# The middle column's product, six units later in a hand-written plan

## The chip, the cores and the metric

The kernel runs on one core of one Trainium2 chip. The metric is the device time of one execution in microseconds (us), the median of the runs shown.

## The reference

Inputs are q, k and v (8 batches, 8 heads, 576 positions, 64 channels, float32) and two feed-forward weights. What is computed:

```python
out_local = softmax(band(q k^T / 8, |i - j| < 4)) v
out_up    = repeat(softmax(qd kd^T / 8) vd, 4)
x     = (out_up + out_local).reshape(8, 576, 512)
mixed = real(fft(fft(x, axis=1), axis=2))
u     = x + mixed
un    = (u - mean(u)) / sqrt(var(u) + 1e-6)
out   = u + relu(un @ w_ch1) @ w_ch2
```

Here qd, kd and vd are means over groups of four positions (144 groups). The Fourier step is what the change touches: its real part is made of matmuls with cosine and sine tables, first along the sequence, then along the channels.

## The kernel before, in words

**Stages.** The work before the feed-forward goes batch by batch. `Unit` (five per batch, 40 in all) does the banded attention: `scores`, `maxima`, `exps`, `transpose_p`, `copy_p`, `values`, `result`. `Pooled` does the pooled attention in three parts per batch, from sums of q and k over four positions (`sum_in`, on VectorE and GpSimd) and sums of v (`sum_v`, on GpSimd, from loads of vsum). `Mix` does the Fourier step. `Block` (nine blocks of four tiles of 128 tokens) adds u together by DMA, normalizes it, turns it and runs the feed-forward; `Quarter` converts the 64-bit weights into pairs of float32r parts, in a chain of a load by SyncE, `size` on ScalarE (L190), `clamp` on GpSimd (L195), `join` on VectorE (L203 to L209), `high` on ScalarE (L220) and `low` on GpSimd or VectorE (L225).

**The Fourier step of a batch (class `Mix`).** The symmetry of the tables lets the kernel fold the channels: `cross` (L649, GpSimd) and `fold` (L659 and L660, VectorE) make sums and differences, `split_high` (L667, ScalarE) and `split_low` (L675, GpSimd, for the last fold VectorE) part each value into two float32r numbers. There are four slots of rows; slot 0 is folded last. `sequence(T)` for T = 0 to 3 (L695) is a wide product: twelve matmuls of 290 columns, of high and low parts of all four slots with the table seqm; slot 0 is the last of each four. `sequence_high` (L703) and `sequence_low` (L706) read its result. These are the four wide products.

The fold leaves out the middle column, number 256 of 512. `split_z` (L680 on VectorE, L683 on ScalarE, L684 on VectorE) puts it into the small tile z, high and low part side by side, so two columns of weights. `sequence_z` (L719) multiplies it with seqm in eight matmuls of 290 columns into a bank of PSUM; `z_high` (L722, ScalarE) and `z_low` (L725, VectorE) write it as rows 0 to 1 and 32 to 33 of the tile yz. The even half of `mix` (L741), the channel stage, reads yz in its last matmul.

**What sets the order.** Nothing is reordered by a compiler. Every step is put on a list with a time in units of a plan, `at(t, step)`; the list is sorted by these times (L1070) and issued in that order, which is the order on each engine's queue. A batch has 20 units (`PACE`). The times come from the table `AT` (L28 to L67); for the Fourier step they count from `mix_at(b)`, stretched by 1.21 for batch 0:

```python
            for d, fn in zip(AT["z"], (self.split_z, self.sequence_z, self.z_high, self.z_low)):
                at(t + pace * d, fn)
```

With `"sequence": (12.86, 2.15, 0.71, 1.85)` the four wide products stand at 12.86, 15.01, 17.16 and 19.31, their readers 0.71 and 1.85 behind each. The first value of `AT["z"]` also enters `t_a` (L988), the time from which the plan closes the attention's memory and starts the feed-forward; for the last batch `t_a` is 9.14 behind `mix_at`, so from there blocks of the feed-forward stand between its wide products.

**Banks of PSUM.** `bank()` (L278) gives each product the bank whose last reader has the earliest time in the plan. There are eight banks before `t_a` and four after it, the other four being the feed-forward's accumulators.

Of the kernel before, what the change touches and what calls it, by code (L numbers as in the profile page):

```python
# [35 lines left out]
    "crosses": ((1, 4.24), (2, 5.87), (0, 8.67)),  # L36
    "folds": ((3, 3.9), (1, 4.66), (2, 7.94), (0, 10.61)),
    "splits": (0.74, 1.58, 2.04),
    "z": (9.04, 9.92, 11.56, 13.75),
    "sequence": (12.86, 2.15, 0.71, 1.85),  # L40
    "mixed": (22.32, 2.54, 0.37, 0.41, 1.73, 2.46),
    "store_local": (6.68,),
# [1172 lines left out]
```

## Time and profile before

| what | value |
|---|---|
| median of 3 runs | 1126.36 us (1123.96 to 1127.71) |
| the profiled execution | 1122.9 us |
| its span | 1121.1 us, 20828 instructions |
| TensorE busy | 1076.5 us (96%) |
| VectorE busy | 527.6 us (47%) |
| ScalarE busy | 346.8 us (31%) |
| GpSimd busy | 347.0 us (31%) |
| mean granted clock of TensorE | 0.977 |

The span is the time from the first to the last instruction of the profiled execution; the rest of its time lies around it. In the profile PE is TensorE, PEld its weight loads, DVE VectorE, ACT ScalarE, POOL GpSimd, SP SyncE. [...] Batches 0 to 7 have their product of the middle column at 52.8, 82.4, 121.8, 162.0, 202.4, 239.1, 272.4 and 301.2 us.

### The profile page before, as it was taken

The numbers are of one execution on the slowest core, as the hardware profiler recorded it, in microseconds if no ns is written. First come the engines' busy times: TensorE is split into PE (matmuls) and PEld (weight loads), VectorE is DVE, ScalarE is ACT, GpSimd is POOL, SyncE is SP. The second block draws the span as 40 slices with busy tenths as digits, with TensorE's granted clock in tenths as the row PEclk, the third lists the DMA queues.
The fourth block names the chain that finished last, engine by engine and source line by source line (L and its number), as shares of the span: only waits on it lengthen the run. The fifth ranks groups of instructions, "written<-read, shape, count | busy, mean of one in ns | idle before, by whom it ended". The sixth has DMA issues, their size and how long they took to land.

```text
span 1121.1 us, 20828 instructions
## 1 busy us (share of the span) xinstructions
PE 1076.5 (96%) x8204; PEld 885.1 (79%) x8204; DVE 527.6 (47%) x1270; ACT 346.8 (31%) x1025; POOL 347.0 (31%) x473
## 2 busy tenths in 40 slices
PE   6899889989899999999999999999999999999998
PEld 5677667768788778888888888888888888888886
DVE  5889699888798884231321322322222232132111
ACT  5877566667444442111111111111111111111110
POOL 3555766664355564205003005004003201300000
PEclk8899799989999999999999999999999999999999
DMA  8777998874434444315007007005104302401001
GB/s 319 266 240 237 248 268 243 224 246 149 132 104 139 121 132 110 61 52 99 1 7 143 1 1 148 4 1 121 30 1 102 49 1 73 78 1 38 1 1 38
DMA packets 67550, 118.50 MB, mean 106 GB/s; under 512 B 8852, under 2 KB 25062, under 8 KB 67451
## 3 DMA queue, kind: packets, MB, share of 16 engines
q1 hardware_dynamic: 50986, 97.22, 26.8%
q0 software_dynamic: 16464, 19.93, 11.5%
q8 instruction: 65, 1.06, 0.4%
q14 instruction: 35, 0.28, 0.1%
HBM read 89.21 MB, written 27.65 MB: 104 GB/s over the span
## 4 chain that ended last, share of the span: by engine, by line
PE 74%; DVE 11%; DMA 6%; ACT 4%; issue 2%; POOL 1%; SPq 1%; ACTq 0%; DVEq 0%; POOLq 0%
PE hps L922 31%; PE acc L942 11%; PE acc L940 11%; PE acc L941 10%; DMA raw<-in_wq_dram 3%; PE y L695 2%; ACT sb L534 1%; PE mix L741 1%; DVE wt L206 1%; PE tpn L890 1%; DMA vsum<-in_vg_dram 1%; PE tpl L546 1%; PE sc L515 1%; PE av L563 1%; DVE mx L528 1%
## 5 line engine op out<-in xcount | busy, mean ns | idle before, releaser
L930 DVE SCALAR_TENSOR_TENSOR hl<-hps,hh 128x512 fp32r<-128x512 f32 x144 | 99.3, 690 | 461.9 <-ACT hh L926 461.9
L922 PE MATMUL hps<-unT,w1h 128*128 128x512 f32 x1152 | 311.4, 392 | 0.0
L922 PEld LDWEIGHTS hps<-unT,w1h 128*128 128x128 f32 x1152 | 215.0, 188 | 43.9
L926 ACT ACTIVATE hh<-hps 128x512 fp32r<-128x512 f32 x144 | 86.0, 598 | 503.9 <-PE hps L922 501.7
L940 PE MATMUL acc<-w2h,hh 128*128 128x512 f32 x576 | 225.5, 392 | 1.8 <-DVE ut L946 0.9
L942 PE MATMUL acc<-w2h,hl 128*128 128x512 f32 x576 | 224.6, 390 | 0.0
L941 PE MATMUL acc<-w2l,hh 128*128 128x512 f32 x576 | 224.2, 389 | 0.0
L922 PE MATMUL hps<-unT,w1l 128*128 128x512 f32 x576 | 154.4, 390 | 0.0
L940 PEld LDWEIGHTS acc<-w2h,hh 128*128 128x128 f32 x576 | 108.0, 188 | 25.1 <-DVE ut L946 1.3
L942 PEld LDWEIGHTS acc<-w2h,hl 128*128 128x128 f32 x576 | 108.1, 188 | 23.7 <-DVE hl L930 1.2
L922 PEld LDWEIGHTS hps<-unT,w1l 128*128 128x128 f32 x576 | 108.3, 188 | 23.1 <-POOL w1l L225 0.2
L941 PEld LDWEIGHTS acc<-w2l,hh 128*128 128x128 f32 x576 | 108.2, 188 | 22.0
L852 POOL DMA_DIRECT2D ut<-um x72 | 61.6, 1492 | 195.9 <-DMA ut<-ul 192.6
L875 POOL TENSOR_TENSOR rstd<-rstd,mhalf 128x1 f32<-128x1 f32 x36 | 20.0, 555 | 277.6 <-DVE rstd L874 275.7
L534 ACT ACTIVATE sb<-sc,mx 128x64 f32<-128x64 f32 x320 | 69.8, 329 | 1.3
L899 DVE TENSOR_TENSOR unT<-tpn,unT 128x512 fp32r<-128x512 f32 x36 | 24.8, 689 | 61.3 <-ACT unT L896 61.3
L332 POOL TENSOR_TENSOR vsum<-vsum 128x650 f32<-128x650 f32 x24 | 38.5, 1603 | 39.6 <-DMA vsum<-in_vg_dram 39.5
L896 ACT CAST unT<-tpn 128x512 fp32r<-128x512 f32 x36 | 21.2, 588 | 94.5 <-PE tpn L890 94.5
L190 ACT ACTIVATE wt<-raw 128x256 f32<-128x256 f32 x64 | 28.2, 441 | 67.7 <-DMA raw<-in_wq_dram 50.6
L695 PE MATMUL y<-seqm,fh 128*128 128x290 f32 (+1 forms) x256 | 43.7, 313 | 1.7 <-ACT fh L667 1.3
L839 POOL DMA_DIRECT2D ut<-ud x40 | 43.1, 1794 | 2.0 <-DMA ut<-um 1.8
L649 POOL TENSOR_TENSOR pq<-x 128x256 f32<-128x256 f32 x48 | 32.2, 700 | 28.5 <-issue 15.6
(110 smaller groups left out, 1344.7 us busy)
## 6 DMA issues: line engine op xcount, KB each, us to landing
qkT<-in_qk_dram SPq DMA_DIRECT2D x40, 512.0 KB
raw<-in_wq_dram SPq DMA_DIRECT2D x64, 256.0 KB
vsum<-in_vg_dram SPq DMA_DIRECT2D x32, 325.0 KB
vaug<-in_vw_dram SPq DMA_DIRECT2D x40, 260.0 KB
out_dram<-ut SPq DMA_DIRECT2D x36, 256.0 KB
ul<-x SPq DMA_DIRECT2D x8, 1024.0 KB
ut<-ud POOLq DMA_DIRECT2D x32, 256.0 KB, 6.2
ut<-um POOLq DMA_DIRECT2D x38, 128.0 KB, 4.5
```

Of the source, the lines that this page charges most:

```text
L332: eng.tensor_tensor(out=b, in0=a, in1=b, op=ALU.add)
L534: nc.scalar.activation(out=self.sb[:, hp, h2], in_=sc[:, hp], func=AF.Exp, scale=0.125, bias=self.mx[:, h2, hp : hp + 1],)
L649: nc.gpsimd.tensor_tensor(out=pq[:, i], in0=u[:, t, HD + 1 : DM + 1], in1=v[:, t, 0:HD], op=ALU.add)
L695: nc.tensor.matmul(y, l, r, start=(i == 0), stop=(i == len(mms) - 1))
L839: nc.gpsimd.dma_start(out=u[to : to + m], in_=groups, accum_op=ALU.add)
L852: nc.gpsimd.dma_start(out=u[to : to + m, h * HD : h * HD + HD], in_=um[b][i, k + j : k + j + m, z : z + HD], accum_op=ALU.add,)
L922: nc.tensor.matmul(hps, a[:, c, :], unT[:, x, c, :], start=(i == 0), stop=(i == len(mms) - 1))
L926: nc.scalar.activation(out=hh, in_=self.hps[f], func=AF.Relu)
L930: nc.vector.scalar_tensor_tensor(out=hl, in0=self.hps[f], scalar=0.0, in1=self.hh[f].bitcast(F32), op0=ALU.max, op1=ALU.subtract)
L940: nc.tensor.matmul(acc, hh, w2h, start=start, stop=False)
L941: nc.tensor.matmul(acc, hh, w2l, start=False, stop=False)
L942: nc.tensor.matmul(acc, hl, w2h, start=False, stop=stop)
```

## The change

Of the table `AT` the second, third and fourth time of "z" change. `sequence_z` moves from 9.92 to 15.8, `z_high` from 11.56 to 16.8 and `z_low` from 13.75 to 17.3; `split_z` keeps 9.04.

```diff
     "splits": (0.74, 1.58, 2.04),
-    "z": (9.04, 9.92, 11.56, 13.75),
+    "z": (9.04, 15.8, 16.8, 17.3),
     "sequence": (12.86, 2.15, 0.71, 1.85),
```

In each batch the eight matmuls of L719 then come between the second wide product (15.01) and the third (17.16), where they came ahead of the first (12.86). On ScalarE L722 comes behind the second wide product's L703 and ahead of the exponentials of the unit numbered 3 (L531, L534); on VectorE L725 comes between the second and the third wide product's L706. In the last batch the first wide product is preceded by one block's `first(0)` (twelve matmuls of 512 columns, L922), which also stood behind the middle column's product and now follows what was ahead of that.

## Rows read from the trace of the kernel before

**Rows 1.** Busy time by stretch: us, engines' busy us, granted clock, DMA share, GB/s

```profile
150.00:200.00 50.00, 43.82 (x766) 34.45 (x758) 47.02 (x141) 36.83 (x136) 31.34 (x42) 0.97 0.84 261
500.00:550.00 50.00, 50.00 (x226) 41.40 (x225) 11.32 (x23) 6.46 (x11) 16.28 (x20) 1.00 0.40 78
```

**Rows 2.** Waits of TensorE, 0 to 345 us: total us, times, longest us

```profile
PE tpl L546 <- ACT sb L534: 9.6, 9, 4.0
PE yz L719 <- DVE z L684: 9.2, 5, 4.2
```

**Rows 3.** Timeline of TensorE, batch 2: start us, us, [idle before <- releaser]

```profile
121.80 2.09 PE L719 MATMUL yz<-seqm,z 128*2 128x290 f32 x8 [4.18 <-DVE z L684]
...
138.71 1.31 PE L695 MATMUL y<-seqm,fh 128*128 128x290 f32 x8
```

**Rows 4.** Timeline of ScalarE, batch 2

```profile
116.93 0.22 ACT L531 ACTIVATE mx<-mx 128x8 f32<-128x8 f32 x1
117.19 1.74 ACT L534 ACTIVATE sb<-sc,mx 128x64 f32<-128x64 f32 x8
...
123.93 0.39 ACT L722 CAST yz<-yz 2x290 fp32r<-2x290 f32 x1 [2.78 <-PE yz L719]
```

**Rows 5.** Timeline of VectorE, batch 2

```profile
119.05 2.61 DVE L684 TENSOR_TENSOR z<-zf,z 128x4 fp32r<-128x4 f32 x1 [1.45 <-ACT z L683]
...
123.86 0.41 DVE L660 TENSOR_TENSOR xeo<-pq 128x256 f32<-128x256 f32 x1
126.02 0.76 DVE L528 TENSOR_REDUCE mx<-sc 128x4 f32<-128x256 f32 x2 [1.74 <-PE sc L515]
126.69 0.68 DVE L675 TENSOR_TENSOR fl<-xeo,fh 128x512 fp32r<-128x512 f32 x1
```

**Rows 6.** Busy time by stretch: batches 2, 5 and 7 (columns as above)

```profile
116.00:136.00 20.00, 15.76 (x202) 12.27 (x201) 12.41 (x33) 10.28 (x36) 15.93 (x22) 0.66 0.96 222
...
236.00:252.00 16.00, 14.39 (x208) 11.57 (x209) 12.56 (x34) 9.55 (x35) 9.20 (x15) 0.79 0.73 194
298.00:316.00 18.00, 13.87 (x72) 11.32 (x71) 13.34 (x24) 6.68 (x17) 8.85 (x13) 0.91 0.66 197
```

**Rows 7.** Chain of waits, batch 6: start us, us, what

```profile
272.43 1.17 PE yz L719 x8
...
277.35 1.83 PE y L695 x12
...
284.37 1.66 PE y L695 x12
286.03 0.70 PE av L563 x32
```

**Rows 8.** Timeline of ScalarE, batch 7

```profile
306.06 0.43 ACT L190 ACTIVATE wt<-raw 128x256 f32<-128x256 f32 x1 [4.69 <-DMA raw<-in_wq_dram]
...
307.80 0.61 ACT L667 CAST fh<-xeo 128x512 fp32r<-128x512 f32 x1
```

**Rows 9.** Timeline of TensorE, batch 3

```profile
170.73 0.40 PE L695 MATMUL y<-seqm,fl 128*128 128x290 f32 x1 [1.11 <-DVE fl L675]
```

**Rows 10.** Timeline of VectorE, batch 4

```profile
206.38 0.76 DVE L528 TENSOR_REDUCE mx<-sc 128x4 f32<-128x256 f32 x2 [0.60 <-PE sc L515]
```

**Rows 11.** Timeline of TensorE, batch 5

```profile
239.07 2.09 PE L719 MATMUL yz<-seqm,z 128*2 128x290 f32 x8 [0.78 <-DVE z L684]
```

**Rows 12.** Chain of waits, one block of the feed-forward

```profile
431.77 2.72 PE hps L922 x12
```

**Rows 13.** Timeline of TensorE, batch 7

```profile
301.22 1.85 PE L719 MATMUL yz<-seqm,z 128*2 128x290 f32 x8 [2.86 <-DVE z L684]
```

**Rows 14.** Busy time by stretch: 375 to 410 us

```profile
375.00:410.00 35.00, 33.18 (x142) 25.99 (x141) 29.34 (x60) 15.01 (x39) 20.48 (x33) 1.00 0.43 125
```

**Rows 15.** Chain of waits, 185 to 240 us

```profile
220.31 5.65 DMA vsum<-in_vg_dram
```

**Rows 16.** Timeline of GpSimd, batch 2

```profile
139.94 0.55 POOL L497 TENSOR_TENSOR two<-qkT 128x216 f32<-128x216 f32 x1 [3.09 <-DMA qkT<-in_qk_dram]
```

## The prediction

> **What bounds the kernel now.** I read the busy time by stretch first. From 500 us on TensorE has no gap (50.00 of 50 us), while VectorE has 11.32 [rows 1]. So the last 700 us are a fixed queue of matmuls, and every microsecond by which TensorE enters that queue sooner or later moves the end by one, unless a wait on the way gives it back. Ahead of it, in 150 to 200 us, VectorE is the fuller engine (47.02 us against TensorE's 43.82) [rows 1]. Then the waits of TensorE: the second largest group up to 345 us is the middle column's product (L719) waiting for its operand z, written by VectorE in L684: 9.2 us in five waits, the longest 4.2 [rows 2]. These waits are what the change can touch.
>
> **The mechanism, at batch 2.** The product starts at 121.80 after 4.18 us without work [rows 3]. TensorE issues in order, so the transposes and scores queued behind it waited too, though the exponentials that they need were done at 117.19 + 1.74 = 118.93 [rows 4]. The operand was late for a reason that the move leaves alone: L684 itself took 2.61 us on VectorE [rows 5]. The wait costs a second time through the clock. [...]
>
> **The change, part by part.** Per batch three steps change their place: eight matmuls with their weight loads on TensorE, one copy on ScalarE (L722, 0.39 us [rows 4]) and one subtraction on VectorE (L725). Nothing is added or removed, no step moved issues a DMA, and no step goes past anything on SyncE's or GpSimd's queue. split_z keeps its time, so t_a and every later block of the plan stay. The product's bank of PSUM is held for 1.5 units of the plan instead of 3.83; the next reader of its result, the even mix, comes 5.4 units after z_low, so nobody waits for it.
>
> *The price where it goes.* At full clock, batch 6, the product takes 1.17 us [rows 7]. Moved into an unbroken stretch it costs that there and saves that where it was: batches 0, 1 and 6, which hardly wait now, come out at 0 (ends: -0.2 and +0.3 each).
>
> *Batch 2.* Free of the product, TensorE goes on at 118.93. In batch 6 the work from the product's end (272.43 + 1.17 = 273.60) to the first wide product (277.35) took 3.75 us [rows 7], so that one starts at 122.7. Its fourth matmul needs the last fold's high part: fold done at 123.86 + 0.41 = 124.27 [rows 5], copy of 0.61 us [rows 8], so 124.9. The last matmul needs the low part: the maxima (L528), which now sat waiting 1.74 us for scores, follow the fold directly, then 0.68 us of L675 [rows 5]: 125.6, in time. Three of twelve matmuls (1.83 / 12 = 0.15 us each) are done by then; the other nine take 1.4 us, the way from the first to the third wide product another 284.37 - 279.18 = 5.2 [rows 7], and the product 1.2. The third wide product starts at 132.7 instead of 138.71 [rows 3]: 6.0 us earlier at full clock. The two waits that stay (1.3 and 1.8 us) can still lower the clock. With one lower stretch as short as batch 7's, 3.3 us at half speed, 1.7 is lost and 4.3 gained; if the clock stayed low until 134.4 as now, 1.2 would be left. I take **-4.3** (ends -6.0 and -1.2), since its two waits are each nearer to batch 7's 2.86 us than to 4.18.
>
> *Batch 3.* TensorE also waits before the product, but the first wide product then stands 1.11 us for L675 [rows 9] behind a VectorE that is full [rows 1]. That gate does not move: 0 (ends -0.5 and +1.2, the product's own time).
>
> *Batch 4.* The scores come forward, and the maxima's 0.60 us wait for them [rows 10] goes: -0.5 (ends -1.0 and +0.2).
>
> *Batch 5.* 0.78 us of waiting goes [rows 11], but the clock is already low there, so the work that moves up runs at half speed, while the product now pays 1.2 us of full speed elsewhere: -0.5 (ends -1.5 and 0).
>
> *Batch 7* is the debit. Here the product and one block of the feed-forward (2.72 us [rows 12]) fill the time until the last fold's high part. That copy (L667) stands in ScalarE's queue behind weight conversions, the first of which waited 4.69 us for its load and started at 306.06; the copy ends at 307.80 + 0.61 = 308.4 [rows 8], or 308.1 with L722 (0.3 of ScalarE's time) gone from ahead of it. The product began after 2.86 us of waiting, so TensorE was free at 298.36 [rows 13]. It would now do the block by 301.1 and three matmuls by 301.5, then stand **6.6 us**. After the gate it has 1.2 us more to do (the product), 0.3 gained by the earlier gate, and 1.7 lost at the lower clock if the stretch is again 3.3 us: +2.6. From 375 to 410 us TensorE still loses 35.00 - 33.18 = 1.8 us to weight conversion [rows 14], waits that shrink when TensorE comes later; conversion is itself held in part by TensorE's results in the same queues, so I count 1.0 of it back: **+1.6** (ends 0 and +7).
>
> [...]
>
> *ScalarE's queue at the new place.* The copy L722 now stands ahead of unit 3's exponentials, which so start after the product. Copy, scaling and exponentials are 0.4 + 0.2 + 1.74 = 2.3 us [rows 4]; TensorE meanwhile has the third wide product and the values, 1.66 + 0.70 = 2.4 [rows 7], before it needs them. Cost 0, covered by 0.1 us; without that cover 0.3 per batch (end +2.4). L725 moves to where VectorE waits for TensorE's values anyway: 0.
>
> Sum: -4.3 - 0.5 - 0.5 + 1.6 = **-3.7 us**.
>
> **Against the times.** The profiled execution took 1122.9 us with a span of 1121.1; it lies 3.5 below the median of 1126.36. The sum gives 1119.2 for an execution like the profiled one and **1122.7** for the median. About 0.3%, 3.4 us, is what a measurement here can tell from no change, so the forecast is just beyond it.
>
> **The rivals.**
>
> *A: as summed.* Batch 2's gain reaches the matmul queue: 1122.7, between -9.6 (all good ends together) and -3.4. For it: past batch 5 the chain of waits is TensorE's own work [rows 7], and of TensorE's two largest waits neither ends on a load [rows 2]. Chance 0.43.
>
> *B: the gain stops at VectorE and the loads.* From 150 to 200 us VectorE is nearly full [rows 1]; later the chain of waits runs over a load of vsum of 5.65 us [rows 15], and GpSimd's key sums waited 3.09 us for a load at 139.94 [rows 16], just ahead of the next pooled scores. If those loads or VectorE's own work can't come sooner, batch 2 gives 1 us instead of 4.3 and the sum is -0.4: 1126.0, range -3.4 to +3.4. Against it: the load at 139.94 is released by TensorE's scores, so it comes sooner with them. Chance 0.37.
>
> *C: slower, through batch 7's stand.* Place: from 301.5 to 308.1 us. If after 6.6 us of standing the clock stays low as long as after batch 2's 4.18 (13.6 us), 6.8 us are lost instead of 1.7; with the product's 1.2, less 0.3, that is +7.7. From there on TensorE has no slack but the 1.8 us. With 1.0 given back it costs 6.7, and so it decides, slower by over 3.4, as soon as the batches before keep less than 3.3; with batch 2 at its low end (-1.2) and the two halves the sum is -2.2 + 6.7 = +4.5: 1130.9. Against it: after 2.86 us at this very place the clock was low for 3.2 us only. Chance 0.20.
>
> That the plan would not do what it says is no rival: the new times sort between the second (15.01) and third (17.16) wide product in every batch, batch 7 included.
>
> **The numbers.** Faster 0.43, within 0.3% 0.37, slower 0.20. The range 1116.8 to 1130.5 reaches from A's good ends together (-9.6) through B nearly to C's time, which leaves out part of C and little else; A alone would be 1116.8 to 1123.0.
>
> **What would show it.** Right: the wait of L719 for L684 gone from TensorE's list; the mean clock of the 20 us around batch 2's first wide product above 0.8; the third wide product of batch 2 some 4 us earlier and batch 6's still 3 to 5 earlier; then a stand of 5 to 7 us on L695 for L667 at batch 7, the largest of the phase, with a low clock behind it. B shows as an earlier batch 2 but a batch 4 or 6 at the old times; C as a clock low for over 6 us after batch 7's stand. Wrong altogether if L719 waits at its new place, if the transposes (L546) wait longer for L534 in every batch, or if batch 7's copy L667 comes much earlier than 308 less the gain before it.

## The result, and the profile after

The changed kernel takes 1131.24 us (median of 7 runs, 1130.47 to 1134.78) against 1123.76 (7 runs) of the kernel before in the same series: ratio 1.0076, 95% interval 1.0052 to 1.0099. That is some 8.5 us slower (by the ratio), outside the forecast's range. The profiled execution is the median one (1131.24 us, span 1129.5; before 1121.1).

Busy time by stretch of the kernel after; columns as in [rows 1]:

```profile
150.00:200.00 50.00, 43.92 (x731) 35.82 (x730) 47.43 (x132) 34.66 (x127) 30.52 (x41) 0.92 0.77 233
500.00:550.00 50.00, 50.00 (x224) 41.42 (x223) 12.21 (x23) 5.87 (x10) 15.75 (x19) 1.00 0.42 85
...
50.00:70.00 20.00, 17.94 (x279) 14.14 (x277) 16.25 (x50) 11.22 (x39) 9.74 (x16) 0.83 0.57 183
140.00:152.00 12.00, 9.37 (x141) 8.23 (x132) 8.62 (x23) 4.88 (x19) 7.60 (x10) 0.72 1.08 306
158.00:178.00 20.00, 16.69 (x278) 13.44 (x278) 18.16 (x56) 13.16 (x47) 15.23 (x23) 0.83 0.75 216
306.00:322.00 16.00, 9.51 (x45) 8.13 (x44) 11.32 (x24) 6.81 (x18) 7.73 (x13) 0.79 0.61 177
116.00:136.00 20.00, 16.67 (x248) 13.65 (x238) 16.04 (x44) 11.13 (x38) 17.36 (x24) 0.83 0.94 234
```

The granted clock is a share of full speed. In windows of 1 us the two profiled executions show 1.00 (1060 of 1121 windows before, 1059 of 1129 after) or 0.50 (45 and 52), the few others lie between; in batch 2 of the kernel before it is 1.00 up to 120 us and 0.50 from 121 to 134. So a mean gives the time at the lower clock, 2 x (1 - mean) x length: 13.6 us for the 0.66 and 3.2 us for the 0.91 of [rows 6].

The last 700 us are the same full queue of matmuls (50.00 of 50 us busy in both, and from the third wide product of batch 7 to the end 807.1 us, before 807.0), so the loss lies ahead of it. Batch 2's clock rose as forecast (0.66 in [rows 6], now 0.83), but four other stretches are low, among them those of batches 0 and 7, which had 0.94 and 1.00 before (same view, the kernel before; the other two, 140 to 152 and 158 to 178 us, had 1.00 and 0.91):

```profile
50.00:70.00 20.00, 19.65 (x326) 15.66 (x324) 17.46 (x56) 13.21 (x48) 9.42 (x17) 0.94 0.53 174
306.00:322.00 16.00, 14.73 (x85) 13.07 (x84) 13.85 (x28) 8.69 (x24) 8.72 (x15) 1.00 0.42 128
```

The waits of TensorE after, 0 to 460 us (total us, times, longest):

```profile
PE tpl L546 <- ACT sb L534: 11.1, 10, 4.1
PE y L695 <- ACT fh L667: 6.5, 2, 6.3
...
PE avd L400 <- DVE x L582: 2.6, 3, 1.9
PE avd L400 <- DVE o L753: 2.5, 1, 2.5
```

L719's 9.2 us for z [rows 2] are gone. L695 now waits for L667 (6.3 us at once), and L400, which starts a new PSUM bank, waits for the bank's last reader, L582 or L753. Where the rest of the time goes is read from one point in each batch, the start of the third wide product (L695, third block of the batch in TensorE's timeline). The moved product lies ahead of that point in both kernels.

| batch | before, us | after, us | later by |
|---|---|---|---|
| 0 | 66.19 | 70.04 | 3.9 |
| 1 | 95.34 | 98.65 | 3.3 |
| 2 | 138.71 | 137.91 | -0.8 |
| 3 | 176.15 | 180.98 | 4.8 |
| 4 | 215.37 | 220.54 | 5.2 |
| 5 | 252.46 | 256.96 | 4.5 |
| 6 | 284.18 | 289.42 | 5.2 |
| 7 | 314.13 | 322.37 | 8.2 |

Four steps, then: batch 0 loses 3.9, batch 2 gains 4.1, batch 3 gives it all back and 1.5 more, batch 7 loses 3.0. TensorE's timeline of the kernel after shows the place of each:

```profile
51.83 0.70 PE L563 MATMUL av<-vaug,pT 64*64 64x65 f32 x32
54.30 0.94 PE L546 MATMUL tpl<-ident,sb 128*128 128x128 f32 x4 [1.77 <-ACT sb L534]
...
56.88 1.97 PE L413 MATMUL avd<-vsum,ptd 128*128 128x65 f32 x8
...
125.35 0.81 PE L400 MATMUL avd<-vd,ptd 64*128 64x130 f32 x4 [2.52 <-DVE o L753]
...
143.26 0.48 PE L351 MATMUL sp<-sums 64*32 64x144 f32 x16 [1.64 <-POOL sums L498]
144.73 2.27 PE L695 MATMUL y<-seqm,fh 128*128 128x290 f32 x8 [0.99 <-DVE x L582]
...
167.83 0.47 PE L400 MATMUL avd<-vd,ptd 64*128 64x130 f32 x2 [1.92 <-DVE x L582]
...
313.49 1.58 PE L695 MATMUL y<-seqm,fh 128*128 128x290 f32 x5 [6.25 <-ACT fh L667]
315.83 2.13 PE L695 MATMUL y<-seqm,fh 128*128 128x290 f32 x8
```

In batch 0 the kernel before had the product in that gap, and L546 came without a wait:

```profile
52.83 1.23 PE L719 MATMUL yz<-seqm,z 128*2 128x290 f32 x8
53.99 0.70 PE L563 MATMUL av<-vaug,pT 64*64 64x65 f32 x32
54.66 0.94 PE L546 MATMUL tpl<-ident,sb 128*128 128x128 f32 x4
```

L413's eight matmuls behind the bared wait take 1.97 us, at a clock of 0.50; those of the kernel before, at 57.01 us, take 1.11 at 1.00. Batch 2 gains its 4 us although L400 now stands 2.52 us there for a bank, and begins to lose them at the next pooled scores: L351 waits for key sums, and these (VectorE's timeline, after) for loads of keys:

```profile
139.97 0.66 DVE L500 TENSOR_REDUCE sums<-qkT 128x120 f32<-128x480 f32 x1 [1.73 <-DMA qkT<-in_qk_dram]
142.10 0.60 DVE L500 TENSOR_REDUCE sums<-qkT 128x108 f32<-128x432 f32 x1 [1.48 <-DMA qkT<-in_qk_dram]
```

The chain of waits after, 130 to 150 us, runs over that load (start us, us, what): TensorE's scores free its buffer, it takes 8.26 us, and the clock drops behind the wait (0.72 in 140 to 152 us).

```profile
133.26 0.55 PE sc L515 x32
133.81 0.02 issue
133.82 8.26 DMA qkT<-in_qk_dram
142.08 0.02 issue
142.10 0.60 DVE sums L500
```

The same two loads in the kernel before (SyncE's timeline) were issued 7.2 us apart, in the changed kernel 2.0 (131.78 and 133.8 us):

```profile
128.46 0.46 SPq L480 DMA_DIRECT2D qkT<-in_qk_dram  x1
...
135.70 0.33 SPq L480 DMA_DIRECT2D qkT<-in_qk_dram  x1
```

There the second had landed when GpSimd used it at 139.94 us [rows 16], 4.2 us behind its issue.

### The profile page after: what moved, and what is told of

Same layout as the page of the kernel before. It is cut to its first block, busy times and chain, and to the rows that moved or that the text cites. A ratio compares the mean times of both kernels' runs of the same rounds, so it can differ in the third digit from the quotient of the medians.

```text
span 1129.5 us, 20832 instructions
## 1 busy us (share of the span) xinstructions
PE 1079.8 (96%) x8204; PEld 889.9 (79%) x8204; DVE 527.7 (47%) x1270; ACT 347.6 (31%) x1025; POOL 346.9 (31%) x473
## 4 chain that ended last, share of the span: by engine, by line
PE 76%; DVE 11%; DMA 5%; ACT 4%; issue 2%; POOL 1%; SPq 1%; ACTq 0%; DVEq 0%; POOLq 0%
PE hps L922 31%; PE acc L942 11%; PE acc L940 10%; PE acc L941 10%; PE y L695 4%; DMA raw<-in_wq_dram 3%; DMA qkT<-in_qk_dram 1%; PE avd L413 1%; ACT sb L534 1%; PE mix L741 1%; PE tpn L890 1%; DVE x L582 1%; PE av L563 1%; DVE sums L500 1%; DVE mx L528 1%
## 5 line engine op out<-in xcount | busy, mean ns | idle before, releaser
L922 PE MATMUL hps<-unT,w1h 128*128 128x512 f32 x1152 | 310.3, 391 | 0.0
L922 PEld LDWEIGHTS hps<-unT,w1h 128*128 128x128 f32 x1152 | 214.3, 188 | 43.7 <-ACT w1h L220 0.2
L922 PE MATMUL hps<-unT,w1l 128*128 128x512 f32 x576 | 154.3, 390 | 0.0
L922 PEld LDWEIGHTS hps<-unT,w1l 128*128 128x128 f32 x576 | 108.1, 188 | 23.2 <-POOL w1l L225 0.3
L534 ACT ACTIVATE sb<-sc,mx 128x64 f32<-128x64 f32 x320 | 70.0, 330 | 1.3
L695 PE MATMUL y<-seqm,fh 128*128 128x290 f32 (+1 forms) x256 | 48.5, 337 | 8.5 <-ACT fh L667 6.5
L695 PEld LDWEIGHTS y<-seqm,fh 128*128 128x128 f32 (+1 forms) x256 | 41.1, 216 | 13.5 <-ACT fh L667 7.1
L839 POOL DMA_DIRECT2D ut<-ud x40 | 43.8, 1827 | 1.9 <-DMA ut<-um 1.4
```

What stands on the lines that cost most here:

```text
L534: nc.scalar.activation(out=self.sb[:, hp, h2], in_=sc[:, hp], func=AF.Exp, scale=0.125, bias=self.mx[:, h2, hp : hp + 1],)
L695: nc.tensor.matmul(y, l, r, start=(i == 0), stop=(i == len(mms) - 1))
L839: nc.gpsimd.dma_start(out=u[to : to + m], in_=groups, accum_op=ALU.add)
L922: nc.tensor.matmul(hps, a[:, c, :], unT[:, x, c, :], start=(i == 0), stop=(i == len(mms) - 1))
```

## Experiments

Three theories of the loss. *Cover and clock*: at its old place the product filled waits of batches 0 and 7; bared, they stop TensorE and lower its clock (0.83 in 50 to 70 us, 0.79 in 306 to 322 us). *Loads*: what batch 2 gains stops at the key sums, which wait for loads of keys. *Banks*: the move gives other products other PSUM banks, whose last readers come late.

**1. Which batches.** The time of the steps per batch is chosen from a list, the three kernels differ only in it (shown: batch 2 alone):

```diff
+EARLY, LATE = (9.04, 9.92, 11.56, 13.75), AT["z"]
+Z_OF = [EARLY, EARLY, LATE, EARLY, EARLY, EARLY, EARLY, EARLY]
-            for d, fn in zip(AT["z"], (self.split_z, ...
+            for d, fn in zip(Z_OF[self.b], (self.split_z, ...
```

*Late in batches 1 to 6.* 

> The product late in batches 1 to 6, at its old place in batches 0 and 7. Cover theory (where the product stood it filled waits of TensorE, and its going opens them in batches 0 and 7): the 3.9 us of batch 0 and the 3.0 us of batch 7 stay away, so +0 to +3 us against the kernel before, the waits of L546 at 54 us and of L695 for L667 at 313 us gone. Bank theory (the shifted rotation of PSUM's banks makes products wait for readers): the waits of L400 in batches 2 and 3 stay, +5 to +8 us. Load theory (what batch 2 gains it loses at the key loads): a wait of L351 of 1 to 3 us ahead of batch 2's fourth wide product, whatever the total.

Measured: 1125.01 us, ratio 1.0024 (1.0006 to 1.0043). The waits at 54 and 313 us are gone. L351 stands only 0.29 us for the sums, less than the load theory said, and 3.3 of batch 2's 3.6 us are left there (it starts 43.8 us after batch 1's point, before 47.1). Most of them go in batch 3, where L400 stands 1.93 us for a bank and the clock is 0.78 from 170 to 178 us (1.00 before): its point comes 80.7 us after batch 1's, before 80.8.

*Late in batch 2 alone.* 

> The product late in batch 2 alone. Forecast of the prediction: the third wide product of batch 2 some 4 us earlier, and the end 3 to 4 us earlier. Load theory: the third wide product 3 to 4 us earlier, then L351 waits 1 to 3 us for the key sums, the clock falls, and the fourth wide product and all after it stand at the old times, so -1 to +2 us. Cover theory says nothing against the gain: -3 to -4. Bank theory: L400 waits 2 to 3 us behind the scores, which leaves 1 to 2 us of gain at the third wide product.

Measured: 1123.33 us, ratio 1.0002 (0.9982 to 1.0021). From batch 1's point to batch 2's it takes 39.4 us against 43.4 before (4.0 gained), to batch 3's 80.65 against 80.81: nothing is left. L351 stands 1.46 us for the sums there.

*Late in batches 0 and 7 alone.* 

> The product late in batches 0 and 7 alone. Cover theory: L546 waits 1.5 to 2 us for the exponentials in batch 0 and L695 some 6 us for L667 in batch 7, the clock falls behind each; +6 to +7.5 us against the kernel before. Bank theory: the loss sits in batches 2 and 3, so +0 to +2 here unless the rotation shifted in batch 0 makes later products wait. Load theory: +0 to +1.

Measured: 1128.11 us, ratio 1.0052 (1.0031 to 1.0073). Both stands are there, 1.83 and 6.38 us. So batches 0 and 7 make 5.8 of the 8.5 us, the six others 2.7, and the two add up, as far as intervals of some 2 us to each side can tell. This run shows one thing more. In batch 2, where nothing was moved, TensorE came 4.2 us sooner than in the execution of before (39.2 us from point to point), and then it stood for the key sums:

```profile
145.56 0.74 PE L351 MATMUL sp<-sums 64*32 64x144 f32 x16 [4.18 <-POOL sums L498]
```

Batch 3's point came 84.0 us after batch 1's, 3.2 later than before.

**2. The banks.** The whole change, where a list worked out from the times of before gives each other product its bank of before, but for five and the product itself.

```diff
     def bank(name, rows=P):
-        free = min(banks)
+        free = every[kept[key, turns[key]]]
```

> The whole change, but every other product keeps the bank of PSUM that it had before the change (five of them and the product itself take another). Bank theory: the waits of L400 for L753 and L582 in batches 2 and 3 (2.5 and 1.9 us) go with the low clock behind them, 4 to 7 us less than the changed kernel, so +0 to +4 against the kernel before. Cover theory: batches 0 and 7 keep their losses, at least +6. Load theory: the wait for the key sums in batch 2 grows to 3 to 4 us, since TensorE comes there sooner, and the end is at +5 to +8.

Measured: 1139.59 us, ratio 1.0149 (1.0117 to 1.0181): a miss. Its waits of TensorE (the lines of this kernel stand 65 later, so L611 is L546, L574 is L509):

```profile
PE tpl L611 <- ACT sb L599: 10.2, 11, 3.8
PE y L760 <- ACT fh L732: 6.5, 2, 6.2
PE tpl L611 <- DVE x L647: 3.6, 2, 2.1
PE sc L574 <- DVE o L818: 2.8, 1, 2.8
```

The waits for bank readers don't vanish, they meet other products, and harder: this kernel is some 8 us slower than the changed one. So going back to the old banks is not the cure, and the run doesn't tell what the new ones cost. The other traces show that the new waits belong to the move. L400 stands 2.5 us in batch 2 in all seven kernels with the planner's own banks and batch 2's product at the late place, 1.9 us in batch 3 in all five with batch 3's product moved, and 0.47 us in batch 6 in all four with batch 6's moved:

```profile
279.25 0.46 PE L400 MATMUL avd<-vd,ptd 64*128 64x130 f32 x2 [0.47 <-DVE x L582]
```

(the changed kernel). Where the batch's product is at its old place, L400 waits for no bank longer than 0.25 us. That they explain the 2.7 us of batches 1 to 6 is not shown.

**3. Cover or clock.** Two ways to mend batches 0 and 7 with work that is of no use. First an unread copy of the product at the old place:

```diff
+            if self.b in (0, 7):
+                at(t + pace * 9.92, self.unread)
```

> The whole change (the product late in all eight batches), plus in batches 0 and 7 eight more matmuls on TensorE at the product's old place, whose result nobody reads: work is added, none is taken away. Cover theory: what batches 0 and 7 lost was the product's work at its old place, which filled the wait for batch 0's exponentials (1.8 us) and for batch 7's last copy (6.3 us), and kept the clock up. Then the added work pays for itself: in batch 0 L546 waits under 0.7 us and the third wide product starts at most 1.5 us later than before (3.9 with the change alone); in batch 7 the wait of L695 for L667 is 1 to 2 us shorter, because the added product again stands for z ahead of it and the gap is cut in two; the time is about 1126 to 1128 us, 3 to 5 us above the kernel before and 3 to 5 below the changed kernel. Rival 1 (the loss comes from something else that went with the move, the other PSUM banks or the steps at the new place): the added work only costs, 2 x 1.2 us, and the time is 1133 us or more. Rival 2 (batch 7's loss is the stand for the copy alone, which work ahead of it cannot shorten): batch 0 gains its 3, batch 7 nothing.

Measured: 1126.02 us, ratio 1.0026 (1.0009 to 1.0042): eight matmuls more in each of the two batches, and some 5.5 us less than the change without them. Batch 7's point comes 31.0 us after batch 6's, with the change alone 33.0, before 30.0. In batch 0 L547 (L546 there) follows without a wait:

```profile
52.70 1.23 PE L726 MATMUL yz<-seqm,z 128*2 128x290 f32 x8
53.85 0.82 PE L564 MATMUL av<-vaug,pT 64*64 64x65 f32 x32
54.60 0.86 PE L547 MATMUL tpl<-ident,sb 128*128 128x128 f32 x4
```

From the copy's start to the third wide product (67.23) it takes 14.5 us, the 13.4 of before (52.83 to 66.19) and the copy's own time, where the change alone takes 18.2.

Second, matmuls that leave each stand as long as it is but keep TensorE at work in it:

```diff
+            for _ in range(10 if (self.b, self.m) == (1, 2) else 0):
+                nc.tensor.transpose(tp[:, :P], ident, ident)
...
+            for _ in range(36 if self.b == 7 and T == 0 else 0):
+                nc.tensor.matmul(y, *mms[0], start=True, stop=True)
```

> The whole change, plus matmuls without use in the two stands: ten 128x128 transposes of the identity ahead of batch 0's transposes that wait for the exponentials, and 36 matmuls of 290 columns after the first part of batch 7's first wide product, whose result the next matmul overwrites. The stands' lengths stay (TensorE can't go on sooner), only what TensorE does in them differs. Clock theory: about half of the loss in batches 0 and 7 is the lower clock after the stand (6.8 us at half speed, 3.4 us each). Then the granted clock behind both stands is 0.9 or more, the third wide product of batch 0 starts 2 to 3 us sooner than with the change alone and that of batch 7 2 to 4 us sooner, and the time is 4 to 6 us below the changed kernel's, 1126 to 1128 us. Stand theory: the loss is the stand itself and the work that must follow it; the clock costs nothing that the work behind would not give back; the time is within 1.5 us of the changed kernel's, 1130 to 1133.

Measured: 1127.04 us, ratio 1.0027 (1.0005 to 1.005), again some 5.5 us less. The 36 stand ahead of the first three matmuls of the first wide product, not behind them as the expectation has it; the time without work that they fill is the same. Its windows:

```profile
50.00:70.00 20.00, 19.13 (x335) 15.27 (x334) 16.72 (x55) 14.02 (x53) 10.42 (x18) 1.00 0.60 197
...
306.00:322.00 16.00, 13.78 (x79) 12.46 (x79) 11.04 (x25) 7.74 (x21) 7.83 (x13) 0.89 0.56 151
```

Batch 0, from the values ahead of the wait (L563, 51.83 after, 52.35 here) to the third wide product (70.04; 67.58): 18.2 and 15.2 us. Before, from the product's start, 13.4. So batch 0 costs 4.9 us (the table's 3.9, because this execution came to the place 1.0 us earlier), 1.9 of it the stand (1.77) and 3.0 the clock. In batch 7 the 36 matmuls ran out 2.2 us too soon, the clock fell again behind that rest (eight matmuls of L699 take 2.13 us at 312.60 and 1.25 at 319.27), and from batch 6's point to batch 7's it takes 32.6 us, hardly less than the 33.0 of the change: a miss there, run 4 decides it. So at the two places this trace shows 3.4 of the 5.5 us; where the others come from it doesn't show.

**4. The kernel before, its stands filled.** No step moves; useless matmuls of 2x290 stand ahead of the product, 28 in batch 2 and 18 in batch 7.

```diff
+            for _ in range({2: 28, 7: 18}.get(self.b, 0)):
+                nc.tensor.matmul(y, seqm[:, 0, 0, 0, :2], seqm[:, 0, 0, 0, :], start=True, stop=True)
```

> The kernel before, with matmuls without use (2x290 columns, overwritten by the product itself) right ahead of the product, 28 in batch 2 and 18 in batch 7, about as long as the stands for z there (4.2 and 2.9 us). No step moves. Clock theory: of batch 2's 13.6 us at the lower clock some 6 are given back at once, the third wide product of batch 2 starts 3 to 6 us sooner. Load theory (rival B of the prediction): whatever batch 2 gains is lost again at the next key sums and the loads of qkT, vsum, and batch 3's third wide product starts within 1.5 us of before; only batch 7's clock, 1.6 us, can reach the end. Time by the load theory 1121 to 1123 us, by the clock theory alone 1117 to 1119 us, with 1122.8 before.

Measured: 1125.65 us, ratio 1.0026 (1.0004 to 1.0049). The clock of 116 to 136 us is 1.00, and batch 2's point is reached 38.1 us after batch 1's, 5.3 sooner than before, with the product at its old place (kernels without any fill differ here as well, see below). 3.1 of them are lost by batch 3. The time is above what either theory said, 1117 to 1123. In batch 7 TensorE, earlier now, stands for the same copy as in the changed kernel:

```profile
307.01 1.58 PE L695 MATMUL y<-seqm,fh 128*128 128x290 f32 x5 [3.79 <-ACT fh L667]
```

With 25 more matmuls for this stand, ahead of the first wide product (not behind its third matmul, as the expectation has it):

> The kernel before with the useless matmuls ahead of the product in batches 2 and 7 (28 and 18) as before, and 25 more after the third matmul of batch 7's first wide product, where the run with two fills stood 3.8 us for the last copy at the lower clock. Clock theory for batch 7: the granted clock from 305 to 320 us is 0.95 or more, the product after the stand runs at full clock, the third wide product of batch 7 starts 1.5 to 3 us sooner than with two fills (33.4 us after batch 6's, then 30.5 to 32), and the time is 1120 to 1123 us, at or a little under the kernel before. If batch 7's loss lies in the copy alone, 33 us stay and the time is 1124 to 1126.

Measured: 1122.76 us, ratio 1.0002 (0.9979 to 1.0024). The clock of 305 to 320 us goes from 0.77 (two fills) to 1.00 (three):

```profile
305.00:320.00 15.00, 12.99 (x62) 12.02 (x62) 13.26 (x28) 7.94 (x22) 8.43 (x14) 0.77 0.38 108
```

```profile
305.00:320.00 15.00, 14.86 (x86) 13.22 (x85) 13.96 (x29) 8.18 (x22) 8.53 (x14) 1.00 0.40 109
```

and from batch 6's point to batch 7's it takes 30.6 us instead of 33.4. The stand is what the copy makes it. Its end came 0.4 us sooner (24.9 us after batch 6's point, with two fills 25.2); from there to the third wide product it takes 5.7 us instead of 8.1, and these 2.4 us are the clock.

**5. Another place.** In batches 2 to 5 right ahead of the first wide product (12.5, 13.2, 13.9 units), early in the others.

```diff
+EARLY, MID = (9.04, 9.92, 11.56, 13.75), (9.04, 12.5, 13.2, 13.9)
+Z_OF = [EARLY, EARLY, MID, MID, MID, MID, EARLY, EARLY]
```

> In batches 2 to 5 the product comes right ahead of the first wide product (12.5 units instead of 9.92; copy at 13.2, subtraction at 13.9); batches 0, 1, 6 and 7 as before. TensorE no longer waits for z ahead of the transposes and scores, but the product still stands between them and the wide products, whose folds (batch 3) come late. If the loss of the late product in batches 3 to 5 is the product missing as cover ahead of the first wide product, this keeps it: batch 3's third wide product is not later than before and the time is 1119 to 1122 us. By the load theory batch 2's 4 us are again lost by batch 3 and the time is within 2 us of before, 1121 to 1125. If each changed order of banks brings new waits whatever the place, it is 1125 or more.

Measured: 1126.18 us, ratio 1.0014 (0.9995 to 1.0033). Batch 2 gains 4.7 us, then L351 stands 5.24 us for the key sums, and batch 3's point comes 84.8 us after batch 1's, 4 later than before. The hope for 1119 to 1122 us fell.

**6. The loads.** Two loads of keys and queries (512 KB each) are left out, once with the product early, once late in batch 2.

```diff
+            if self.u in (18, 19):
+                self.qkT = loaded[17]
+                return
```

> The kernel before, without two loads of keys and queries: the fourth and fifth unit of batch 3 read the third one's tile again, so that two transfers of 512 KB fall away (the output changes; no engine's work does). It is the control for the next run. Load theory: in before the loads issued at 128 to 137 us gate the key sums (GpSimd waits 4.0 us for qkT), but batch 2's TensorE is late anyway through z and the clock, so the third wide product of batch 3 starts 0 to 2 us earlier, counted from that of batch 1 (80.8 us in before). If instead it starts over 3 us earlier, the loads alone bound the phase already in the kernel before.

> The product late in batch 2 alone, and the same two loads left out. Load theory: batch 2's gain of 4.0 us (41.4 us from batch 1's third wide product to batch 2's with the loads in, 39.4 without the stand) is no longer lost at the key sums; the wait of L351 for the sums (1.5 us) is under 0.5 us, and batch 3's third wide product starts 2.5 to 4 us earlier, counted from batch 1, than in the control with the product early. VectorE theory (rival to the load: VectorE's own work between the batches is full, and takes the gain back whatever the loads do): less than 1 us earlier than the control. The time stands 1 to 4 us below the control's by the load theory as far as batch 7's copy lets it through, within 1 by the other.

Measured: 1121.12 us (ratio 0.9970, 0.9949 to 0.9992) and 1120.25 us (0.9980, 0.9961 to 0.9998). Batch 3's point came 80.3 and 79.3 us after batch 1's, a difference of 1.1 where the load theory had 2.5 to 4 (its 41.4 us with the loads in are 43.4 in the trace), and L351 still stood for the sums, 3.8 and 0.8 us. The runs tell little of that wait: the loads left out are those that the kernel before issued at 86 and 92 us, and the sums stood for loads issued at 127 to 131 us, which are batch 4's. With those left out instead (units 23 and 24):

> The kernel before, in which the fourth and fifth unit of batch 4 read the third one's tile of keys and queries again (two loads of 512 KB, issued at 128 us, fall away; the output changes, no engine's work does). Control for the next run. Load theory: the wait of the key sums at 134 to 140 us is gone, but TensorE is late through z and the clock, so batch 3's third wide product comes 0.5 to 2.5 us sooner, counted from that of batch 1 (80.8 us in before).

> The product late in batch 2 alone, and the same two loads left out. Load theory: L351's wait for the sums (1.5 us) and the sums' waits for qkT (1.7 and 1.5 us) are gone, batch 2's 4 us stay, and batch 3's third wide product starts 1.5 to 4 us sooner than in the control, counted from batch 1 (about 77 against 79 us); the fourth wide product of batch 2 no longer waits for VectorE. VectorE theory: the sums come sooner and the products still start where the control has them, within 1 us. The time is 1 to 3 us below the control's by the first, within 1 by the second.

Measured: 1123.50 us (0.9985, 0.9961 to 1.0010) and 1121.28 us (0.9975, 0.9954 to 0.9995). With the product late, L351 and the fourth wide product (L699 is L695) no longer wait:

```profile
140.84 0.48 PE L351 MATMUL sp<-sums 64*32 64x144 f32 x16
141.25 1.33 PE L699 MATMUL y<-seqm,fh 128*128 128x290 f32 x8
```

```profile
141.94 0.48 PE L351 MATMUL sp<-sums 64*32 64x144 f32 x16 [1.46 <-POOL sums L498]
143.41 2.18 PE L695 MATMUL y<-seqm,fh 128*128 128x290 f32 x8 [0.98 <-DVE x L582]
```

The second fence is the kernel with the product late in batch 2 alone, loads in. Batch 3's point, counted from batch 1's, comes at 76.9 us against 80.65 there, and at 79.0 in the control. So in these executions the late product does better without the loads: the stand at L351 is gone, and 2.1 us stay against the control, as the load theory said. The times are too close to confirm it (their intervals overlap), and the 2.1 us are no more than kernels with the product early differ by at this point (80.3 to 84.0 with these loads in). At batch 2's own point the two don't differ (40.0 and 40.1 us), which neither theory said. The control's rows tell why, its timeline and its window:

```profile
121.28 2.09 PE L723 MATMUL yz<-seqm,z 128*2 128x290 f32 x8 [4.18 <-DVE z L688]
```

```profile
116.00:136.00 20.00, 15.76 (x224) 12.85 (x221) 15.24 (x43) 12.10 (x46) 16.45 (x23) 0.83 0.98 228
```

It stood for z exactly as long as the kernel before [rows 3], and its clock was 0.83 where [rows 6] have 0.66: 6.8 us at the lower clock instead of 13.6, an estimate with 0.50 as the lower clock here too, which is 3.4 us of time, with nothing moved. It was up again soon after 126 us (L413's eight matmuls at 126.11 take 1.14 us), ahead of the 128.5 at which the kernel before issues the first of the loads left out.

## Why the prediction was wrong

The sum was -3.7, and up to batch 7's point the changed kernel is 8.2 us later. Of the 12 us between, batch 3 makes 5.6, batch 0 3.9 (both were forecast at 0) and batch 7 1.4. Two steps failed: that nothing is lost where the product goes away from batch 0, and that what batch 2 gains lasts.

*Batches 0, 1 and 6 at 0: a step that failed.* It holds for 1 (-0.5 from one batch's point to the next). Batch 6 cost 0.7, small but no chance: 32.45 to 32.47 us in the four kernels with its product late, 31.69 to 31.72 in the ten with it early, and the former have L400's bank wait of 0.47. Batch 0 cost 3.9 (4.9 from its own start). The step asked what the product waits for, and it hardly waits there. It did not ask what the product covers: L546 behind it waits for exponentials (L534) that come 1.8 us later than TensorE without the product. The prediction named such waits, "in every batch", as a sign that would make it wrong altogether, and priced them nowhere. Run 3 shows it from both sides: with the product's work put back batch 0 takes 3.7 us less and batch 7 2.0, which is what the whole time gained (some 5.5); with other work in the stand batch 0 takes 3.0 less.

*Batch 2 at -4.3.* Measured -4.1, and yet the term was not sound. It compares the 13.6 us of low clock of one execution with 3.3, batch 7's 3.2 of [rows 6] carried over; behind the waits that batch 2 had in the changed kernel (0.75 us for exponentials, 2.52 for a bank) the clock was low for 6.8 us (0.83 of 20). From batch 1's point to batch 2's the four kernels with the product early there and no fill take 43.4 (before), 39.2 (late in batches 0 and 7 alone), 37.5 and 40.0 us (the controls, with loads left out), those with it late and the planner's own banks 38.3 to 40.1. The move removes the wait for z and brings L400's bank wait of 2.5 us, which the prediction did not have; most of the 4 us came from a clock that stayed low for a long time in the execution that was read. That the number came out is luck.

*That it lasts: the other step that failed.* Rival B named the place (key sums, a load of qkT released by scores) and priced it at 1 us left of 4.3; nothing was left. The objection to B, "it comes sooner with them", holds for the issue alone: counted from batch 1's point the load was issued 5.2 us sooner (35.2 instead of 40.4), but it landed only some 1.2 sooner, because it took 8.26 us instead of 4.2. That it followed the other load more closely is the likely reason, not tested. From there an estimate accounts for batch 3's 5.6 us: stands of 1.64 and 0.99 us and 3.4 us for 12 us at a clock of 0.72 (1.00 before) make 6.0. But the load is not the only thing that takes the gain: in batches 1 to 6 alone it is lost with hardly a stand at L351, behind L400's bank wait in batch 3. The term for batch 3, 0, left out that a changed order changes who gets which bank; it has a wait of 1.92 us there and a window of 0.83 instead of 0.91. And in the kernel with the product late in batches 0 and 7 alone a gain in batch 2 was lost at the key sums with no product moved there at all. How the 5.6 us divide between loads and banks stays open.

*Batches 4 and 5, -0.5 each.* Measured +0.3 and -0.7. Within what one execution can tell.

*Batch 7 at +1.6.* The mechanism was right to the line, the stand 6.25 us where 6.6 was forecast. The size was off: 3.0. The last copy (ScalarE's timeline, after; [rows 8] have it at 307.80) ends at 313.43, 24.0 us after batch 6's point, 0.2 sooner than before:

```profile
312.83 0.60 ACT L667 CAST fh<-xeo 128x512 fp32r<-128x512 f32 x1
```

From its end to the third wide product it takes 8.9 us instead of 5.7: 1.2 for the product and some 2 for the clock, where 1.7 was forecast. The clock was low for 6.7 us (0.79 of 16), twice the 3.3 of the forecast, but only 4.9 of them (0.73 of the 9 us from 313.4) lie behind the copy; in the stand a low clock costs nothing. The larger error is the 1.0 counted back: nothing of it is seen, 8.2 us at batch 7's point are 8.4 at the end. A longer stand did come with a lower clock (306 to 322 us: 1.00 before, 0.79 with the stand; 305 to 320 us in run 4: 0.77, and 1.00 with work in the stand), but the larger end, +7, no run shows.

*The rivals.* The time came out beside C's 1130.9, but that is chance: C's figure is 4.5 above the median of 1126.36 that the forecast started from, the measured loss 8.5 above the 1123.76 of the same series. Nor was it by C: batch 7's clock stayed low half as long as C said (6.7 us, not 13.6), and batch 0, which C did not have, cost more than batch 7. That batch 2's gain is lost is B's forecast; of B's causes the trace shows the loads, beside banks that B did not have. The tail is as said: TensorE full (50.00 of 50 us), and the 8.2 us at its entry are 8.4 at the end.

## What to carry to other kernels

Ahead of moving work away from a place, ask of the place itself what it covers: take the work out of the timeline, let the engine go on, and see what it meets next and when that is ready. The short wait bared in batch 0 cost its length, 1.9 us, and then the lower clock behind it, the larger part (3.0 of 4.9 us). And a gain at one point is followed to the next transfer that it can't hurry, and to the next bank: here the 4.1 us of batch 2 did not outlive batch 3.

None of the versions that do all the work beats the kernel before by more than the measurement can tell.

## What was not expected of the hardware

The same stand had no fixed price. After 4.18 us without work at the same instruction the clock was low for 13.6 us in one kernel's execution and 6.8 in another's. It shows in plain repeats too: of 23 runs of the kernel before in the last series the fastest took 1119.2 us at a mean granted clock of 0.982, the slowest 1129.1 at 0.971. 0.011 of 1120 us is 12 us of full-speed time, an estimate, and more than the whole spread of 9.9. A term of a sum that rests on the clock of one profiled execution was uncertain here by several us from that alone.

Useless matmuls paid for themselves twice: in the changed kernel 36 and ten of them came with some 5.5 us less in all, and in run 4 25 in a stand that lasts anyway brought 2.4 us at that place. There the stand hardly ended sooner (24.9 us after batch 6's point, with two fills 25.2), but the work behind it ran at full clock (1.00 instead of 0.77 in 305 to 320 us). It is no rule: the 28 and 18 in the kernel before left it at 1.0026 (1.0004 to 1.0049), and all three fills together at 1.0002.
